# Reading the general-path flag in the middle of the FFN and storing the last output tiles from the SyncE queue

## The chip, the cores and the metric

The kernel runs on one core of one Trainium2 chip. The metric is device time in microseconds (us). One trace of a run has a **span**, from its first to its last record; a timed run is about 1.8 us longer than its span (before: 1277.37 and 1275.6).

The change can only act on a few microseconds out of 1276. So the document relies on one more measure, the **tail**: the time from the start of VectorE's write of the last output tile to the end of the span. It is read from single instruction records of a trace, which have a resolution of about 0.01 us.

## The reference, cut to what matters

One transformer block on 2048 tokens: adaLN modulation, attention of 32 query heads over a cache of 512 keys, and a SwiGLU FFN.

```python
h = _layernorm(x) * (1 + ca) + sa
x = x + ga * _A_ref(h, A_k_cache, A_v_cache, A_wq, A_wo)     # attention, softmax over 512 keys
h = _layernorm(x) * (1 + cb) + sb
x = x + gb * _B_ref(h, B_w_gate, B_w_up, B_w_down)           # silu(h Wg) * (h Wu), times Wd
return x                                                     # (1, 2048, 1024) bf16
```

## The kernel before

The kernel is two programs. The **fast path** takes exponentials without a running maximum, which is safe while a bound on the scores holds. It computes that bound and leaves a flag, 0 if the bound holds. After the fast path every engine reads the flag into a register and branches: with 0 it skips the **general path**, a second complete kernel of over 16,000 instructions on TensorE alone, and meets the others at the end. With these inputs the flag is 0.

```python
    # bound_final(), in the first steps of the FFN: the flag is complete at 681.6 us of 1275.6
        nc.vector.tensor_copy(out=flag, in_=r[:, 7:8])
    # ... cut ...
    def emit_down(cc, dh, t, widths=(512,)):
        row = (cc * QT + t) * P
        c0 = 0
        for w in widths:
            # ... cut: matmuls into d_ps, r = d_ps * gb ...
            o = wk.tile([P, w], BF16, name="o_sb", tag="row", bufs=5)
            nc.vector.tensor_tensor(out=o, in0=r, in1=xt[cc * QT + t][:, dsl], op=ALU.add)
            nc.scalar.dma_start(out=out2d[row:row + P, dsl], in_=o)      # every store: ScalarE queue
            c0 += w
    # ... cut: for cc in range(4): gate/up, then down in two halves dh of four tiles t;
    #          the very last tile is split into widths 256, 128, 128 ...

def tile_adaLN_cond__sliding_block_cached__swiglu_ffn__prompt_kernel(tc, *args):
    nc = tc.nc
    with tc.tile_pool(name="guard", bufs=1) as gp:
        flag = gp.tile([1, 1], I32, name="flag")
        fast_path(tc, flag, *args)
        over = nc.values_load(flag[0:1, 0:1], min_val=0, max_val=1)      # read on every engine
        with tc.If(over > 0):
            general_path(tc, *args)
```

## Time and profile before

| what | value | where it is read |
|---|---|---|
| time, first three runs | 1277.75 us median (1277.31 to 1277.92) | timed runs |
| span of the trace, mean granted clock | 1275.6 us, 0.999 | head of the profile, cores view |
| TensorE busy | 98% of the span | busy table |
| TensorE waits from 690 us on | none | view of waits |
| last write of an output tile starts | 1269.61 us | timeline |
| tail | 5.98 us, 0.5% of the span | end of span less the line above |

The head and the chain of waits of the profile before (the chain follows the last work back through what released it):

```profile
span 1275.6 us, 17906 instructions
...
PE 1255.9 (98%) x7396; PEld 640.6 (50%) x7537; DVE 606.9 (48%) x1325; ACT 333.7 (26%) x433; POOL 1.3 (0%) x10
...
PE 96%; SPq 2%; issue 1%; DVE 1%; DMA 0%
```

TensorE sets the pace until its last matmul. A change of reads and queues can win only in the tail, or lose by disturbing TensorE.

The flag reads of before, by source line. The columns are: line, the engine's queue, operation, operands, count, duration in ns (min/median/max), start of first and last in us:

```profile
L1255 SPq TENSOR_LOAD <-flag x1: 474/474/474, 681.6 to 681.6; - x1
L1255 POOLq TENSOR_LOAD <-flag x1: 497/497/497, 681.6 to 681.6; - x1
...
L1255 PEldq TENSOR_LOAD <-flag x1: 484/484/484, 1268.1 to 1268.1; - x1
L1255 DVEq TENSOR_LOAD <-flag x1: 581/581/581, 1269.6 to 1269.6; - x1
L1255 ACTq TENSOR_LOAD <-flag x1: 477/477/477, 1271.3 to 1271.3; - x1
```

The scheduler had already moved the reads of SyncE (SP) and GpSimd (POOL) to the moment when the flag was ready. TensorE, VectorE and ScalarE read at the end.

The branches of before, and the first record that each engine has after its branch (columns as above):

```profile
L1256 SPq EVENT_SEMAPHORE  x8: 17/17/17, 1260.2 to 1272.9; - x8
...
L1256 SPq COMPARE_BRANCH  x1: 53/53/53, 1241.1 to 1241.1; - x1
L1256 PEldq COMPARE_BRANCH  x1: 3706/3706/3706, 1268.7 to 1268.7; - x1
L1256 DVEq COMPARE_BRANCH  x1: 76/76/76, 1270.3 to 1270.3; - x1
L1256 ACTq COMPARE_BRANCH  x1: 54/54/54, 1271.9 to 1271.9; - x1
L1256 PEldq EVENT_SEMAPHORE  x1: 51/51/51, 1272.5 to 1272.5; - x1
L1256 DVEq EVENT_SEMAPHORE  x1: 21/21/21, 1273.2 to 1273.2; - x1
L1256 ACTq EVENT_SEMAPHORE  x1: 17/17/17, 1274.6 to 1274.6; - x1
```

A branch record itself is short, 0.05 us on ScalarE, but ScalarE has no record from 1271.9 to 1274.6. VectorE has the same hole, from 1270.3 to 1273.2. SyncE branched at 1241.1, thirty microseconds before it was needed. Its eight semaphore records, and twelve more in front of the final barrier, are **joins**: with each it waits until DMA queues or engines are done. The last sixteen follow one another every 0.064 us, from which all twenty are estimated at 1.3 us.

The barrier of before, at which all engines wait for one another, SyncE's part; the third duration is the longest of the fourteen records:

```profile
L1283 SPq EVENT_SEMAPHORE  x14: 17/28/1019, 1273.0 to 1275.5; - x14
```

One of these records lasted 1.019 us, from 1273.66 to 1274.68: SyncE had done everything else and was waiting for ScalarE. So in this trace the tail is ScalarE's chain, in single records: 0.32 us from the write to the issue of the store, 1.35 issue, 0.04 gap, 0.55 from the read of the flag to the branch, 2.77 branch to next record, 0.96 to the end; together 5.98 (summed before rounding).

The output stores of before from 1264 us on:

```profile
L1204 ACTq DMA_DIRECT2D out_dram<-o_sb x4: 338/768/1348, 1264.6 to 1269.9; - x4
```

The last issue took 1.35 us, where most take 0.34.

### The profile page before, as it was taken

Reading aid. Unit: us, or ns where it says so; the run is one execution under the profiler, and the core shown is the slowest. Engines: PE = TensorE matmul, PEld = TensorE weight load, DVE = VectorE, ACT = ScalarE, POOL = GpSimd, SP = SyncE. Lnnn points to the kernel's source line nnn. Section 1 sums busy time; section 2 is a strip of 40 time slices with the busy share of each in tenths; the row PEclk is TensorE's granted clock in tenths of the full one; section 3 lists DMA queues with packets and bytes.
Section 4 is the critical chain, followed back from the end, with each engine's and each line's share of the span. In section 5 each row is a group of like instructions: output and inputs, shape, how many; then the busy total and the mean of one; then the engine's idle time right before and its main releaser. Section 6 shows DMA issues by size and latency. Waiting matters only on the chain.

```text
span 1275.6 us, 17906 instructions
## 1 busy us (share of the span) xinstructions
PE 1255.9 (98%) x7396; PEld 640.6 (50%) x7537; DVE 606.9 (48%) x1325; ACT 333.7 (26%) x433; POOL 1.3 (0%) x10
## 2 busy tenths in 40 slices
PE   8999999999999999999999999999999999999997
PEld 4555555555555555555554444444444444444444
DVE  4575578867587755576654632321222112221212
ACT  4543334343343433333341111011100111011100
POOL 0000000000000000000000000000000000000000
PEclk9999999999999999999999999999999999999999
DMA  9988556685646563546465367426632565425711
GB/s 276 220 219 212 144 137 182 165 192 148 176 125 168 137 183 107 152 112 145 126 196 147 133 226 199 145 95 211 218 129 81 175 216 189 139 91 182 246 35 35
DMA packets 307868, 204.46 MB, mean 160 GB/s; under 512 B 145601, under 2 KB 305345, under 8 KB 307778
## 3 DMA queue, kind: packets, MB, share of 16 engines
q1 hardware_dynamic: 302866, 199.03, 55.0%
q10 hardware_dynamic: 4912, 4.20, 1.0%
q8 instruction: 61, 1.00, 0.3%
q14 instruction: 29, 0.24, 0.1%
HBM read 165.94 MB, written 4.21 MB: 133 GB/s over the span
## 4 chain that ended last, share of the span: by engine, by line
PE 96%; SPq 2%; issue 1%; DVE 1%; DMA 0%
PE gu_ps L1177 30%; PE a_ps L1095 17%; PE q_ps L1018 17%; PE d_ps L1197 15%; PE o_ps L1063 9%; PE s_ps L1031 8%; SPq L664 1%; SPq L703 1%; DMA wq<-in_A_wq_dram 0%; DVE junk L954 0%; DVE qT L915 0%; DVE junk L786 0%; DVE acc L1103 0%; DVE oq L1050 0%; DVE f L1201 0%
## 5 line engine op out<-in xcount | busy, mean ns | idle before, releaser
L1033 ACT ACTIVATE pT<-s_ps 128x1024 bf16<-128x1024 f32 x256 | 248.9, 1020 | 356.6 <-PE s_ps L1031 228.9
L1095 PE MATMUL a_ps<-wo,oT 128*128 128x512 bf16 x987 | 239.9, 379 | 2.0
L1018 PE MATMUL q_ps<-hT,wq 128*128 128x512 bf16 x999 | 236.7, 379 | 0.6 <-DVE modT L755 0.3
L1183 DVE TENSOR_TENSOR guT<-gu_ps,sg 128x512 bf16<-128x512 f32 x112 | 77.4, 691 | 286.4 <-ACT sg L1182 286.4
L1177 PE MATMUL gu_ps<-hT,wg 128*128 128x512 bf16 x875 | 209.7, 379 | 1.1
L1182 ACT ACTIVATE sg<-gu_ps 128x512 bf16<-128x512 f32 x112 | 66.9, 597 | 488.7 <-PE gu_ps L1177 483.0
L1197 PE MATMUL d_ps<-wd,guT 128*128 128x512 bf16 (+2 forms) x934 | 193.2, 366 | 0.9
L915 DVE CAST qT<-q_ps 128x512 bf16<-128x512 f32 x128 | 88.2, 690 | 158.5 <-PE q_ps L1018 157.7
L1177 PE MATMUL gu_ps<-hT,wu 128*128 128x512 bf16 x659 | 162.0, 379 | 0.7
L1095 PEld LDWEIGHTS <-oT 128*128 128x128 bf16 x1024 | 100.1, 98 | 120.6
L1018 PEld LDWEIGHTS <-wq 128*128 128x128 bf16 x1000 | 97.7, 98 | 118.2 <-DMA wq<-in_A_wq_dram 0.7
L1197 PEld LDWEIGHTS <-guT 128*128 128x128 bf16 x952 | 90.9, 98 | 103.0
L1063 PEld LDWEIGHTS <-pT 128*128 128x128 bf16 x2048 | 126.8, 98 | 31.0 <-issue 0.4
L1177 PEld LDWEIGHTS <-wg 128*128 128x128 bf16 x896 | 87.7, 98 | 105.5
L1063 PE MATMUL o_ps<-v_sb,pT 128*128 128x130 bf16 x2048 | 137.3, 220 | 0.1
L1031 PE MATMUL s_ps<-qT,kT 128*128 128x512 bf16 x467 | 129.3, 379 | 3.0 <-ACT pT L1033 0.6
L1177 PEld LDWEIGHTS <-wu 128*128 128x128 bf16 x672 | 65.7, 98 | 79.3
L1050 DVE TENSOR_TENSOR oq<-o_ps,rl 128x256 bf16<-128x256 f32 (+2 forms) x256 | 100.4, 419 | 3.8 <-issue 0.2
L1201 DVE TENSOR_TENSOR f<-d_ps,gb_bc 128x512 f32<-128x512 f32 (+2 forms) x34 | 22.4, 660 | 142.3 <-PE d_ps L1197 142.3
L1031 PEld LDWEIGHTS <-kT 128*128 128x128 bf16 x512 | 44.9, 98 | 31.5 <-issue 1.3
L1103 DVE TENSOR_TENSOR acc<-a_ps,acc 128x512 f32<-128x512 f32 x64 | 44.0, 688 | 34.3 <-PE a_ps L1095 34.3
L1177 PE MATMUL gu_ps<-hT,v_sb 128*128 128x512 bf16 x220 | 56.9, 379 | 0.2
(76 smaller groups left out, 400.2 us busy)
## 6 DMA issues: line engine op xcount, KB each, us to landing
wq<-in_A_wq_dram SPq DMA_DIRECT2D x64, 512.0 KB
wo<-in_A_wo_dram SPq DMA_DIRECT2D x64, 512.0 KB
wg<-in_B_w_gate_dram SPq DMA_DIRECT2D x56, 512.0 KB
wd<-in_B_w_down_dram SPq DMA_DIRECT2D x56, 512.0 KB
wu<-in_B_w_up_dram SPq DMA_DIRECT2D x42, 512.0 KB
v_sb<-in_B_w_up_dram SPq DMA_DIRECT2D x14, 512.0 KB
x<-in_A_x_dram SPq DMA_DIRECT2D x16, 256.0 KB
wm<-in_w_mod_dram SPq DMA_DIRECT2D x4, 1024.0 KB
```

What stands on the lines that cost most here:

```text
L915: nc.vector.tensor_copy(out=t, in_=q_ps)
L1018: nc.tensor.matmul(q_ps, lhsT=wq_tiles[(cc, h // 4, dt // 4)][:, dt % 4, (h % 4) * P:(h % 4 + 1) * P], rhs=hT[("h1", cc)][:, dt, :], start ...
L1031: nc.tensor.matmul(s_ps[:, i, :], lhsT=kT[:, kv, j * P:(j + 1) * P], rhs=qT[g], start=True, stop=True)
L1033: nc.scalar.activation(out=p[:, 2 * jj:2 * jj + 2, :], in_=s_ps, func=ACT.Exp, scale=scale)
L1050: nc.vector.tensor_tensor(out=dst, in0=ps[:, s0:s0 + cnt, 0:Dh], in1=sc, op=ALU.mult)
L1063: nc.tensor.matmul(o_slot["ps"][:, s_, :], lhsT=pT[g][:, j, t * P:(t + 1) * P], rhs=v_sb[:, kv, j, 0:VN], start=(j == 0), stop=(j == WT - 1))
L1095: nc.tensor.matmul(a_ps, lhsT=oT[(cc, 2 * q + i)][:, hh % 4, t * P:(t + 1) * P], rhs=wo_tiles[(cc, q, dh, i)][:, hh % 4, :], start=(hh == ...
L1103: nc.vector.tensor_tensor(out=acc[(cc, t)][:, dsl], in0=a_ps, in1=acc[(cc, t)][:, dsl], op=ALU.add)
L1177: nc.tensor.matmul(ps[:, n, :], lhsT=gu_w[(cc, fg, nm, dt // 4)][:, dt % 4, fi * P:(fi + 1) * P], rhs=hT[("h2", cc)][:, dt, :], start=(dt ...
L1182: nc.scalar.activation(out=g, in_=ps[:, 0, :], func=ACT.Silu)
L1183: nc.vector.tensor_tensor(out=guT[(cc, fg)][:, fi, :], in0=ps[:, 1, :], in1=g, op=ALU.mult)
L1197: nc.tensor.matmul(d_ps, lhsT=guT[(cc, f // 4)][:, f % 4, t * P:(t + 1) * P], rhs=wd_tiles[(cc, dh, f // 4)][:, f % 4, c0:c0 + w], start=( ...
```

## The change

The intent: read the flag long before the end, so that no engine reads it in the tail, and let SyncE, whose queue is empty by then, issue the last four stores (widths 512, 256, 128, 128), so that ScalarE is done earlier.

```diff
-            nc.scalar.dma_start(out=out2d[row:row + P, dsl], in_=o)
+            last = (cc, dh) == (NTC - 1, DH - 1) and t >= QT - 2
+            (nc.sync if last else nc.scalar).dma_start(out=out2d[row:row + P, dsl], in_=o)
@@ in the FFN loop
     for cc in range(NTC):
+        if cc == 1:
+            at_load = len(nc.cur_bb.bb.instructions)
+            over = nc.values_load(flag[0:1, 0:1], min_val=0, max_val=1)
@@ after the loop
+    loads = {}
+    for ins in nc.cur_bb.bb.instructions[at_load:]:
+        if ins.engine not in loads:
+            loads[ins.engine] = ins.name
+        elif loads[ins.engine] and ins.engine != mybir.EngineType.PE:
+            tc.add_manual_dep(
+                ins, loads[ins.engine],
+                mybir.DependencyInfo(mybir.DependencyClass.NoSync, mybir.DependencyReason.DATA),
+                reason="flag is read before the end")
+            loads[ins.engine] = None
+    return over
@@ in the outermost function
-        fast_path(tc, flag, *args)
-        over = nc.values_load(flag[0:1, 0:1], min_val=0, max_val=1)
+        over = fast_path(tc, flag, *args)
```

The manual dependency pins the read ahead of the next instruction on each engine but TensorE, whose read stays at the end. In the built program TensorE's instruction order is otherwise the same. VectorE does eight steps of the last layer norm one output tile earlier, and SyncE has a few weight loads in another order.

## The prediction

> **What bounds the kernel now.** TensorE, until its last matmul: the busy table gives PE 1255.9 us of a 1275.6 us span (98%), the chain of waits gives PE 96%, and granted clock is 0.999. From 690 us on the waits view shows no wait of PE. Only what follows the last matmul (1269.27 us) can move: 6.3 us, 0.5% of the span.
>
> **The tail before, from the instruction records of the last 10 us.** Last output tile written by VectorE at 1269.90. ScalarE issues its store 1269.93 to 1271.28 (1.35 us; 0.34 is usual; an instruction-fetch packet of 1.14 us occupies a DMA engine just then). ScalarE reads the flag (1271.32, 0.48 us), branches (1271.87) and executes nothing until 1274.64: 2.7 us. VectorE's branch (1270.28) to its next record (1273.18): 2.8 us; PE's 3.7 us. An instruction-queue packet starts 0.9 to 1.0 us after each. The Trainium skill ("Runtime: NRT & Kernel Launch", section "Instruction fetch mechanics") says a taken branch beyond the current two-page window forces a DMA fetch first; the trace agrees. The last store has landed by 1272.7 and is not last: SyncE passes its semaphore then, walks 16 more joins at 0.064 us, and waits 1.0 us for ScalarE (1273.66 to 1274.68). Final barrier: 0.9 us. SyncE itself branched at 1241.1, so its fetch was hidden.
>
> **What the change does.** PE's instruction order is the same, and its flag read stays at the end. VectorE, ScalarE and GpSimd read the flag at about 835 us, 0.5 us each, where these idle: off the path. The eight affine steps of the last h2 move one output tile earlier on VectorE and wait for their transpose there, so one down-projection bank is held 6 us longer; four rotate, so PE should not stall. Two weight loads move behind gate/up loads. The last four stores (one 512 wide, then 256, 128, 128) go to SyncE.
>
> - ScalarE: no 0.48 us read; its last store is now at 1252.5, so its branch and refetch are hidden. Gain: it leaves the path.
> - VectorE: reads nothing at the end; branches about 0.6 us earlier, to about 1272.5.
> - SyncE: now issues the last store at 1269.93, slow as before (I assume the same 1.35 us: same engines, same PE fetch), and branches at 1271.3. Its refetch, estimated at 2.75 us from ScalarE and VectorE, ends at 1274.1. Only then can it walk its 20 joins, 20 x 0.064 = 1.3 us, to 1275.4. Barrier 0.9 us: 1276.3.
>
> So 0.5 us of read is removed, but the refetch moves from ScalarE to SyncE, which alone has joins to walk: a loss of about 0.7 us (0.05%). If SyncE's issue takes 0.4 us, a gain of about 0.2.
>
> **Predicted time:** 1278.4 us, 8 in 10 between 1276.8 and 1279.6. Faster by over 2%: 0.005; within 2%: 0.99; slower by over 2%: 0.005.
>
> **What would show each step.** PE's busy time and last matmul end unchanged (1269.3 +/- 0.7). In the last 10 us: no flag read except PE's; SyncE's compare-and-branch at about 1271.3 with its next record about 2.7 us later, then about 20 semaphore records at 0.064 us; ScalarE's branch near 1253. The tail after the last matmul is 7.0 us, not 6.3.
>
> **What would make it wrong.** SyncE's target lying within its fetched page (then about 1276.0); the store issue on SyncE not being held up; PE stalls from the held bank or swapped loads; ordinary scatter (before: 1277.31 to 1277.92), as large as the effect.

## The result, and the profile after

Six runs of each kernel on the same chip: after 1277.93 us median (1277.27 to 1278.88), before 1277.67 us (1275.94 to 1277.92). The ratio is 1.0005, with a 95% interval of 0.9992 to 1.0018: the same within 2%, and not told apart from 1. A ratio here is the mean time of one kernel's runs over the mean of the other's runs of the same rounds, so it is not quite the ratio of the medians.

The head and the chain of the profile after:

```profile
span 1275.4 us, 18052 instructions
...
PE 1263.3 (99%) x7537; PEld 640.6 (50%) x7537; DVE 606.9 (48%) x1325; ACT 333.7 (26%) x433; POOL 1.3 (0%) x10
...
PE 97%; SPq 2%; DVE 1%; DMA 0%; issue 0%
```

The rise in TensorE's busy time, 1255.9 to 1263.3, is no change of the work: the trace before lacks records (7396 matmuls instead of 7537).

The flag reads, branches, barrier and last stores after, in that order of the views (columns as before):

```profile
L1230 DVEq TENSOR_LOAD <-flag x1: 542/542/542, 834.8 to 834.8; - x1
L1230 ACTq TENSOR_LOAD <-flag x1: 474/474/474, 835.9 to 835.9; - x1
L1230 PEldq TENSOR_LOAD <-flag x1: 486/486/486, 1268.2 to 1268.2; - x1
```

```profile
L1270 SPq EVENT_SEMAPHORE  x8: 17/17/17, 1273.2 to 1273.7; - x8
...
L1270 ACTq COMPARE_BRANCH  x1: 54/54/54, 1258.9 to 1258.9; - x1
L1270 ACTq EVENT_SEMAPHORE  x1: 17/17/17, 1261.5 to 1261.5; - x1
...
L1270 DVEq COMPARE_BRANCH  x1: 76/76/76, 1269.7 to 1269.7; - x1
L1270 SPq COMPARE_BRANCH  x1: 53/53/53, 1270.4 to 1270.4; - x1
L1270 DVEq EVENT_SEMAPHORE  x1: 21/21/21, 1272.6 to 1272.6; - x1
```

```profile
L1297 SPq EVENT_SEMAPHORE  x14: 17/28/28, 1273.8 to 1275.4; - x14
```

```profile
L1205 SPq DMA_DIRECT2D out_dram<-o_sb x4: 333/360/542, 1264.6 to 1270.0; - x4
```

The reads of VectorE and ScalarE are gone from the end, as intended. ScalarE branches at 1258.9 and is ready at 1261.5, long before it is needed. But SyncE now branches at 1270.4 instead of 1241.1, has no record until 1273.2, and only then starts on its twenty joins. No join has to wait (they start 0.06 to 0.10 us apart): all others have been ready for a while. In single records: 0.32 to the issue, 0.33 issue, 0.05 gap, 2.82 branch to next record, 1.36 joins, 0.88 to the end; together 5.75 (summed before rounding). The hole after the branch is still on the path. It has only changed engine, and the join walk has come out of its shadow. The store was not far behind, though: its **landing**, the last of the sixteen semaphore counts that report its data as written, came at 1272.55, only 0.64 us before SyncE resumed.

### The profile page after: what moved, and what is told of

It reads as the page before. It is cut to its first block, busy times and chain, and to the rows that moved or that the text cites. A ratio compares the mean times of both kernels' runs of the same rounds, so it can differ in the third digit from the quotient of the medians.

```text
span 1275.4 us, 18052 instructions
## 1 busy us (share of the span) xinstructions
PE 1263.3 (99%) x7537; PEld 640.6 (50%) x7537; DVE 606.9 (48%) x1325; ACT 333.7 (26%) x433; POOL 1.3 (0%) x10
## 4 chain that ended last, share of the span: by engine, by line
PE 97%; SPq 2%; DVE 1%; DMA 0%; issue 0%
PE gu_ps L1177 30%; PE a_ps L1095 17%; PE q_ps L1018 17%; PE d_ps L1197 15%; PE o_ps L1063 9%; PE s_ps L1031 8%; SPq L664 1%; SPq L703 1%; DMA wq<-in_A_wq_dram 0%; DVE junk L954 0%; DVE qT L915 0%; DVE junk L786 0%; DVE acc L1103 0%; DVE oq L1050 0%; DVE f L1201 0%
## 5 line engine op out<-in xcount | busy, mean ns | idle before, releaser
L1201 DVE TENSOR_TENSOR f<-d_ps,gb_bc 128x512 f32<-128x512 f32 (+2 forms) x34 | 22.4, 660 | 141.9 <-PE d_ps L1197 141.9
```

## The experiments

Fourteen traces in all. First what they share. From TensorE's 801st weight load to VectorE's last tile write every trace has 1163.98 or 1163.99 us, whatever was done to reads, loads or stores. So kernels differ in the tail alone; the rest of the scatter lies in the head, the first 105 us. There the traces fall into two groups: in seven the head takes 105.1 to 105.8 us, in the other seven 106.6 to 107.1. The windows view of 20 to 30 us tells the groups apart by the granted clock (column after POOL busy), here for the second and the third trace of the kernel before:

```profile
20.00:30.00 10.00, 9.18 (x54) 3.90 (x51) 4.16 (x9) 4.47 (x6) 0.00 (x0) 0.83 0.81 206
```

```profile
20.00:30.00 10.00, 8.84 (x72) 4.27 (x72) 4.39 (x11) 5.33 (x6) 0.00 (x0) 1.00 0.81 208
```

All seven long heads have 0.83 in this stretch, all seven short ones 1.00. The clock records of the seven show what the mean hides: one piece of 3.41 us at 0.50, beginning between 21.0 and 22.4 us (22.06 in the second trace of before), and 1.00 around it. The two groups' mean heads differ by 1.35 us; an estimate from the clock, half of 3.41 us, is 1.7. Why the clock drops in some executions was not looked into. The kernel before, the whole change, the early read alone and the early read on TensorE too each have traces in both groups, and the effect is larger than what is looked for, so the tails are compared, and timed runs are quoted beside them.

| kernel | issue of last store, us | tail, us | median, us (runs) | ratio to before, 95% interval |
|---|---|---|---|---|
| before, three traces | 1.35, 0.34, 0.34 | 5.98, 4.81, 4.81 | 1277.75 (3), 1276.51 (4), 1277.04 (5) | -, 0.9992, 1.0000 |
| whole change, three traces | 0.33, 0.33, 0.33 | 5.75, 5.81, 5.71 | 1277.93 (6), 1277.38 (5), 1277.99 (5) | 1.0005, 1.0007, 1.0007 |
| early read alone, two traces | 0.34, 0.34 | 4.46, 4.71 | 1277.28 (5), 1277.20 (5) | 1.0002, 1.0000 |
| SyncE stores alone | 0.33 | 5.64 | 1277.68 (5) | 1.0007 |
| stores on GpSimd | 0.54 | 5.07 | 1277.12 (4) | 0.9996 |
| no guard | 0.34 | 2.81 | 1275.30 (5) | 0.9979 (0.9965 to 0.9993) |
| near branch target | 0.33 | 2.83 | 1274.29 (5) | 0.9976 (0.9963 to 0.9990) |
| early read on TensorE too, two traces | 0.79, 0.34 | 4.69, 4.59 | 1276.42 (5), 1277.23 (5) | 0.9994, 1.0002 |

Where no interval is given, it includes 1. The 0.9992 is the kernel before against itself, so a ratio that is off by 0.0007 cannot be told from scatter.

### The early read alone

```diff
 (the whole change, but)
-            last = (cc, dh) == (NTC - 1, DH - 1) and t >= QT - 2
-            (nc.sync if last else nc.scalar).dma_start(out=out2d[row:row + P, dsl], in_=o)
+            nc.scalar.dma_start(out=out2d[row:row + P, dsl], in_=o)
```

> The early flag read alone; all stores stay on ScalarE. 'Tail' is the time from the start of VectorE's write of the last output tile to the end of the span: 5.98 us before, 5.72 after. My theory (the engine that issues the last store must then branch and refetch, 2.7 us; SyncE alone walks some 20 joins of 0.064 us, which are hidden only if it branched early): ScalarE issues the last store in 0.34 or 1.35 us, branches without reading, resumes 2.7 us later, SyncE finds it last, barrier 0.9 us. Tail 4.4 us with a quick issue, 5.4 with a slow one; so 0.5 to 1.5 us less than before, and less than the whole change. Rival (the moved affine steps and reordered loads of the FFN, which this kernel has too, make what difference there is, and the tail does not matter): same time and same tail as the whole change, 5.7.

The tail was 4.46 us with an issue of 0.34: as expected, and 1.3 us below the whole change, against the rival. The branch lines of this trace:

```profile
L1269 SPq EVENT_SEMAPHORE  x8: 17/17/17, 1259.9 to 1272.1; - x8
...
L1269 SPq COMPARE_BRANCH  x1: 53/53/53, 1240.8 to 1240.8; - x1
...
L1269 ACTq COMPARE_BRANCH  x1: 54/54/54, 1270.0 to 1270.0; - x1
...
L1269 ACTq EVENT_SEMAPHORE  x1: 17/17/17, 1272.7 to 1272.7; - x1
```

One step of the theory fell, though: SyncE did not find ScalarE last. It was released at 1271.90 by the landing of the last store, walked its last sixteen joins, and reached ScalarE's at 1272.86, after ScalarE's 1272.70. The end was set by the landing and the walk, with ScalarE's hole just hidden beside them.

The timed runs did not show a gain over before (1.0002). A tail shorter by some tenths cannot be seen there.

> The early read alone, second trace. Theory: 4.4 to 4.5 us of tail with a quick issue, 5.0 to 5.5 with a slow one, always 0.35 to 0.5 less than the kernel before with the same issue time; mean time 1.0 us under the whole change. Rival (the first trace was luck): tail 4.8 us or more with a quick issue.

The second trace had a tail of 4.71 us, a miss of the expected 4.4 to 4.5, and 0.1 instead of 0.35 to 0.5 below before's 4.81. The issue was quick. What was late was the landing: the last store landed at 1273.57, 2.79 us after the write began, where it was 2.55 in the first trace. That 0.24 us is the whole difference of the two tails. In both traces SyncE then walked its last sixteen joins. A 16 KB instruction packet ran from 1270.88 to 1272.23, after TensorE's branch of 1269.9; that it held up the store was not tested. So the early read alone takes the read off the path, and the landing and the walk then end last. Its timed ratio to before was 1.0000. Against the whole change in the same rounds its mean time was lower by 0.82 us the first time and 0.99 the second, as expected (together 0.91, standard error 0.32).

### The SyncE stores alone

```diff
 (the kernel before, and)
-            nc.scalar.dma_start(out=out2d[row:row + P, dsl], in_=o)
+            last = (cc, dh) == (NTC - 1, DH - 1) and t >= QT - 2
+            (nc.sync if last else nc.scalar).dma_start(out=out2d[row:row + P, dsl], in_=o)
```

> The last four stores on the SyncE queue alone; the flag is read where the scheduler put it before. My theory: ScalarE reads and branches after its own last store near 1259 us, hidden; VectorE reads (0.58 us) and resumes near 1273.2, still before SyncE's walk of the joins reaches it; SyncE issues, refetches 2.76 us and walks 20 joins as in the whole change. Tail 5.7 with a quick issue, 6.7 with a slow one: the same as the whole change, within 0.1 us for the same issue time. So the early read is worth nothing once SyncE has the stores. Rival (the flag reads at the end are on the path, and the gain of the change is theirs): tail 0.5 us longer than the whole change, 6.2 or more.

The tail was 5.64 us, within 0.1 of the changed kernel's shortest, 5.71; the rival's 6.2 is ruled out. VectorE still read the flag in the tail (0.54 us) and was ready at 1272.74, before SyncE came to its join at 1273.67. The queue change alone gives the whole change's tail, and the early read is worth nothing beside it.

### A near branch target

The general path is replaced by a chain of six small instructions over all engines (the expectation says five), so that the branch skips almost nothing.

```diff
         with tc.If(over > 0):
-            general_path(tc, *args)
+            # shortened: z = 0 (gpsimd); zp = z @ z (tensor); z1 = zp (vector); z2 = 0 (vector), z2[:, 0:128] = z1 (scalar)
+            nc.sync.dma_start(out=args[-1].flatten_outer_dims()[1920:2048, :], in_=z2)
```

> The whole change, but the general path is replaced by five instructions (wrong on purpose where the flag is set, right on this data, where it is 0), so that every branch target is near. My theory (the 2.7 us between a branch and the next record is the fetch of a far target): every engine resumes within 0.5 us of its branch, as GpSimd does (0.4); no instruction packet in the tail; quick issue; SyncE then waits for the landing of the last store, about 1.7 us after its issue starts (as at 1258.5 before), walks 15 joins, 1.0 us, barrier 0.9: tail about 3.9 us, 1.8 us less than the whole change. Rival (branching and the joins cost 2.7 us wherever the target lies): tail 5.7 us and the same 2.7 us gaps.

The tail was 2.83 us, shorter than expected. The branch lines:

```profile
L1270 DVEq COMPARE_BRANCH  x1: 76/76/76, 1271.1 to 1271.1; - x1
L1270 DVEq EVENT_SEMAPHORE  x1: 21/21/21, 1271.4 to 1271.4; - x1
L1270 SPq COMPARE_BRANCH  x1: 53/53/53, 1271.8 to 1271.8; - x1
L1270 SPq EVENT_SEMAPHORE  x1: 17/17/17, 1272.0 to 1272.0; - x1
```

SyncE goes on after 0.2 us and VectorE after 0.3, and no instruction packet is in the tail. So the 2.8 us hole belongs to the far target and not to branching as such. The expected 3.9 us was too long because the short path needs fewer joins, nine instead of twenty, only three came after the landing, and the store landed 1.46 us after its issue began instead of 1.7. The experiment thus took away hole and walk together; it does not tell their shares, which the records of the whole change do.

### No guard

```diff
         fast_path(tc, flag, *args)
-        over = nc.values_load(flag[0:1, 0:1], min_val=0, max_val=1)
-        with tc.If(over > 0):
-            general_path(tc, *args)
```

> The kernel before without the guarded general path (right on this data; it has no answer for inputs over the bound). It is the floor for any placing of the read and the branch. Theory: no read, no branch, no refetch; SyncE waits for the landing of the last store, 1.8 us after the last write starts as with the near target, a few joins, barrier: tail 2.8 to 3.4 us, so the guard costs 2.6 to 3.2 us in the kernel before. Rival (the tail is mostly the store's landing and the final barrier): tail over 4.5 us.

The tail was 2.81 us. That is the floor: issue, landing, three joins and the barrier. The guard costs the kernel before 2.0 us with a quick issue (4.81 less 2.81) and 3.2 with the slow one. This difference is large enough for the timed runs: ratio 0.9979, which is 2.7 us.

### The stores on GpSimd

GpSimd has 60 instructions in the general path of the built program, and in the traces so far it resumed 0.5 us after its branch began. So its target is taken to be near.

```diff
-            (nc.sync if last else nc.scalar).dma_start(out=out2d[row:row + P, dsl], in_=o)
+            (nc.gpsimd if last else nc.scalar).dma_start(out=out2d[row:row + P, dsl], in_=o)
```

> The whole change with the last four stores on the GpSimd queue, whose branch target is near (it resumed 0.4 us after its branch in every trace). Theory: SyncE and ScalarE branch early and hidden; no far refetch follows the last store except TensorE's, which ends some 3.2 us after the last tile write starts; tail about 4.2 us if GpSimd issues as fast as the others, that is 1.5 us less than the whole change; longer by whatever its issue costs more, which no trace so far shows. Rival (a store at the end costs a refetch of 2.7 us whichever engine issues it): 5.7 us or more.

The tail was 5.07 us, between the theory's 4.2 and the rival's 5.7. The first two lines are its records after the branch and the branch, the third is the issue of its stores:

```profile
L1270 POOLq EVENT_SEMAPHORE  x5: 17/43/1818, 1271.6 to 1273.7; - x5
...
L1270 POOLq COMPARE_BRANCH  x1: 45/45/45, 1271.1 to 1271.1; - x1
```

```profile
L1205 POOL DMA_DIRECT2D out_dram<-o_sb x4: 540/540/682, 1265.8 to 1271.2; - x4
```

GpSimd resumed 0.5 us after its branch, as the theory said. One record then waited 1.82 us, until 1273.6, for the last store, which landed 2.4 us after its issue began at 1271.17. That is no slower than from the other engines: in the nine other traces with the guard and a quick issue the last store landed 2.2 to 2.6 us after its issue began, on ScalarE and SyncE alike. Only in the two traces without a far branch, no guard and near target, did it take 1.5. Which packets or branches lengthen it was not tested.

So the long hole was avoided, but more than half of the expected gain (0.87 of 1.56 us: 5.07 less 4.2, against 5.76 less 4.2) was not reached. The theory had left out what follows the landing: GpSimd's remaining records, then SyncE's last twelve joins, which stood still until 1274.02 and then took 0.75 us, and only then the barrier.

### The kernel before again

> The kernel before, for a second trace. From the second set of traces the stretch from TensorE's 801st weight load to VectorE's last tile write was 1163.99 us in all six kernels, so only the head (the first 105 us) and the tail can differ. Theory: the tail is ScalarE's chain, 0.32 us to the issue, the issue, the read 0.5, the branch and its refetch 2.75, one join and the barrier 0.9: 5.98 us when the issue takes 1.35 us (first trace), 5.0 when it takes 0.34. Rival (the slow issue belongs to this kernel, not to chance): 5.98 again.

The tail was 4.81 us. The sum in single records: 0.32 to the issue, 0.34 issue, 0.04 gap, 0.55 read, 2.60 branch to next record, 0.96 to the end. The last two stores and ScalarE's branch:

```profile
L1204 ACTq DMA_DIRECT2D out_dram<-o_sb x2: 338/370/402, 1269.3 to 1270.9; - x2
```

```profile
L1256 ACTq COMPARE_BRANCH  x1: 54/54/54, 1271.8 to 1271.8; - x1
...
L1256 ACTq EVENT_SEMAPHORE  x1: 17/17/17, 1274.4 to 1274.4; - x1
```

That is the second branch of the expectation, 0.2 us shorter than its 5.0; the rival, 5.98 again, is out.

> Third trace of the kernel before, to see whether its tail is the 4.81 us of the second trace (issue of the last store 0.34 us) or the 5.98 of the first (1.35 us). Theory: the issue is long when packets of the store ahead of it still wait behind TensorE's 16 KB instruction packet, which is chance; the tail is 4.8 plus what the issue takes over 0.34. Rival: the two traces differ by something else in the tail, and a quick issue can come with 5.5 us or more.

Again 4.81 us, with an issue of 0.34. So the 1.35 us issue in the trace that the prediction was made from is not the kernel's usual state. Its cause stays open. The theory said an issue is long when packets of the store ahead still wait; but in five traces (the second and third of the whole change, the second of the early read, the SyncE stores alone, the second of the early read on TensorE too) the store ahead landed 1.4 to 2.0 us after the last issue had ended, and that issue took 0.33 or 0.34. Two of the thirteen last issues on ScalarE or SyncE were long, 1.35 and 0.79, both on ScalarE. SyncE's issues were held up too, but one store earlier: the last but one took 0.54 to 1.08 us in all five traces with SyncE's stores, and ended before the last tile was written, where it cost nothing.

### The changed kernel again

> The changed kernel once more, for a second trace. My theory: SyncE's issue of the last store takes 0.33 us or about 1.35 us, depending on whether the fetch packet of TensorE's branch is on a DMA engine at that moment, and the tail is 5.7 or 6.7 us accordingly; the refetch of SyncE is 2.7 to 2.8 and its walk 1.3 us in either case. Rival: the tail is 5.7 us every time, and the scatter of 1277.3 to 1278.9 us comes from before the last matmul.

The tail was 5.81 us with an issue of 0.33; SyncE's hole was 2.87 and the walk 1.36 us. TensorE's 16 KB packet was on a DMA engine at that moment (it began 0.22 us before the issue and ended 0.97 us after its start), and still the issue was quick, so the theory's condition for a slow issue is refuted. The rival holds for this kernel: the tail is the same, and the scatter comes from the head.

> Third trace of the changed kernel. Theory: tail 5.75 to 5.85 us with a quick issue (0.33 us; both traces so far), about 1 us more than the kernel before has with a quick issue: 2.8 us of refetch and 1.3 us of join walk on SyncE, one after the other. On the same chip and in the same rounds its mean time should be 0.4 to 1.0 us over the kernel before. Rival (no cost at equal issue): tail under 5.2 us.

The tail was 5.71 us, issue 0.33. The span was 1276.8, the longest of the three, because its head was a long one (107.1 us). In all three comparisons the changed kernel was slower by 0.05 to 0.07%, though each interval includes 1. Taking all runs together, over several chips, the means are 1277.09 us for before (42 runs) and 1277.94 for after (16 runs). The difference of 0.85 us has a standard error of 0.22, from standard deviations of 0.85 and 0.73, if all runs are taken as independent. It agrees with the tails: 5.76 less 4.81 is 0.95.

### The early read on TensorE too

```diff
 (the early read alone, and)
-        elif loads[ins.engine] and ins.engine != mybir.EngineType.PE:
+        elif loads[ins.engine]:
```

> The early read alone (stores on ScalarE), and TensorE reads the flag early as well. Theory: TensorE's branch comes 0.5 us earlier, its fetch packet ends before the last store's packets start, the store lands about 0.4 us sooner; but ScalarE's refetch (to 3.4 us after the last write starts) now ends last, so the tail is about 4.35 us against 4.46 of the early read alone: hardly a gain. The read in the middle, 0.49 us on TensorE's sequencer, adds 0 to 0.5 us to the 1163.99 us of the middle, 0 if the sequencer's lead over the array (1.1 us at the end of before) covers it. Rival (TensorE's fetch is what holds the tail): tail 4.0 us or less.

The tail was 4.69 us with an issue of 0.79. TensorE branched at 1268.0, 1.5 us before the last write instead of 0.9. Its read, at 829.8, took 0.67 us, and the middle stayed at 1163.99: it cost nothing. The tail missed the expected 4.35 by the longer issue: ScalarE's next record after its branch, at 1273.20, ended last. The rival's 4.0 was not reached.

> The early read on every engine, second trace; the candidate for the best correct version. Theory: middle 1163.99 us again, so the read on TensorE costs nothing; tail 4.2 to 4.7 us; mean time 1.0 to 1.3 us under the whole change and 0.3 to 0.7 under the kernel before, which is within the scatter of a single run. Rival: as slow as the kernel before.

The tail was 4.59 us with an issue of 0.34; the middle was 1163.99 again. The landing (1273.55) and the walk ended last, as with the early read alone. On another chip the ratio was 1.0002, after 0.9994 the first time; the mean was 0.8 us under the whole change, but 0.2 over the kernel before, where 0.3 to 0.7 under was expected. So of the correct versions this and the early read alone have shorter tails than before by 0.1 to 0.35 us at equal issue, but no run shows either to be faster in time. A version that beats both kernels was not found.

## Why the prediction was right or wrong

The forecast of no change within 2% was right; 1277.93 us lies within 1276.8 to 1279.6 and 0.5 below the point of 1278.4. The range also holds the time of before, 1277.67, so the hit alone says nothing about the mechanism. Point by point:

- **"PE's instruction order is the same ... PE should not stall."** Right. The stretch up to the last write is 1163.98 to 1163.99 us in every trace. The step "one down-projection bank is held 6 us longer" was mis-sized. The reordered loads let SyncE issue the transpose at 806.91 instead of 811.62, so VectorE's wait for it ended at 813.86 instead of 819.50, and the next bank was freed 0.55 us later (816.45 against 815.90). Neither mattered.
- **"VectorE, ScalarE and GpSimd read the flag at about 835 us."** Right for the first two (834.8, 835.9). GpSimd read at 682.7, as before.
- **"its last store is now at 1252.5"** for ScalarE. Wrong by one tile: it is at 1258.6 and the branch at 1258.9. The consequence, a hidden hole, was right (ready at 1261.5).
- **"VectorE ... branches about 0.6 us earlier, to about 1272.5."** Right: 1269.7 and 1272.6. It was not the last before either.
- **"Its refetch, estimated at 2.75 us"** and **"20 joins, 20 x 0.064 = 1.3 us"** on SyncE. Right: 2.82, 2.87 and 2.78 us, and 1.36. The experiment with the near target shows that the hole belongs to the far target. The Trainium skill ("Runtime: NRT & Kernel Launch", section "Instruction fetch mechanics") gives the mechanism, a taken branch beyond the two-page window needs a DMA fetch first; an 8 KB instruction packet 0.9 to 1.4 us after each of these late branches, and none after the near ones, agrees with it.
- **"slow as before (I assume the same 1.35 us ...)."** This term of the sum failed. SyncE's issue took 0.33 us in all three traces. The 1.35 was a chance of the one trace of before that the sum was built on, and the reason that the prediction gave for it, TensorE's fetch, does not hold: that packet began 0.18 us before the slow issue, and 0.19 to 0.22 us before the last issue in seven traces where it was quick. The term entered twice: as a cost of after, predicted at 1276.3 us of span and measured at 1275.4; and silently as the baseline, where the usual tail is 4.81 and not 5.98. Because it stood on both sides it dropped out of the difference; that the sign came out right owes something to this.
- **"a loss of about 0.7 us".** Right in sign, and near in size when kernels with the same issue time are compared: 5.75 less 4.81 is 0.95 us before rounding. From the two sums of records, the read saves 0.55, the walk adds 1.36, the longer hole adds 0.22, and the remaining gaps take off 0.08. The two traces that happened to be made first differ by 0.23 us the other way (5.98 and 5.75), which the prediction's alternative, "a gain of about 0.2", had foreseen for a quick issue. A reader of these two alone would have called the change a small gain.

So half a microsecond of flag read did leave the end, but this alone shortened the tail by only 0.10 and 0.35 us (the early read alone), because SyncE then still waits for the landing and walks. In the whole change it was outweighed because the last store makes its issuing engine branch late, and SyncE is the one engine with twenty joins to do after its branch. Before, those joins ran while ScalarE was in its hole.

The Trainium skill ("DMA: Bandwidth & Descriptors", section "Issuing engines are not separate DMA queues") says that DMAs started from the scalar, sync or gpsimd engine run on the same 16 DMA engines, and that starting them on several engines at once saves only the sequencer's time for the issue. These runs fit: the quick issue takes 0.34 us on ScalarE and 0.33 on SyncE, and with the guard the last store landed 2.2 to 2.6 us after its issue began from all three engines. No view used here shows which DMA engines carried it.

## What to carry to other kernels

Before moving the last transfer to an idle engine, list what that engine must still do after it: here a far branch of 2.8 us and twenty joins of 1.36 us together, both free only as long as the engine ran ahead. When the stake is a thousandth of the time, split the trace into parts that repeat to 0.01 us and compare those, and take a second trace of the baseline before building a sum on it: one chance issue of 1.35 us turned the sign here.

## What the Trainium skill lacked or had wrong

- "Runtime: NRT & Kernel Launch", "Instruction fetch mechanics", gives no duration for the stall of a far branch. These traces: 2.5 to 2.9 us from branch to next record on ScalarE and SyncE, 2.9 to 3.3 on VectorE, a branch record of 3.5 to 4.05 us on TensorE, and 0.2 to 0.3 us on SyncE and VectorE when the target is near.
- The same section has instructions refilled in 16 KiB blocks. Here one instruction queue, whose total fits TensorE's program, moved packets of 16384 bytes (61 of them); the other moved its blocks in packets of 8192.
- "Advanced Engine Details and Errata", "Control Flow Timing", gives 108 ns for a compare-and-branch. Off TensorE the records here are 45 to 76 ns, and the cost is in the hole after them, which that section does not mention.
- "DMA: Bandwidth & Descriptors", "Latency and other measured facts", gives a floor of about 600 ns for a register load. Here most of them took 0.47 to 0.58 us.
- No page has the cost of the joins at the end of a program: 0.06 to 0.10 us each, 1.36 us for the twenty that follow a guarded path on SyncE.
